# Mixer work of a fused attention and mixer kernel: eight single bursts into four double ones, and low-rank sums at another place

## The chip, the cores and the metric

One core of one Trainium2 chip. The metric is device time of one launch in microseconds (us); the kernel before takes 1078.82 us, the median of 3 runs (1078.75 to 1081.77; with the fourth run that came with the result, 1079.48). The gate for "faster" or "slower" is 2%.

## The reference

Two parts, one after the other, for 8 batches of 3136 rows and 256 columns, float32 in and out:

```python
scores = (1.0 / S) * np.matmul(z, z.transpose(0, 2, 1))   # z: 3136 x 64
out    = u * np.matmul(np.maximum(scores, 0.0) ** 2, v)   # attention
x      = out
h      = x.transpose(0, 2, 1) @ U @ V                     # mixer: rank 32 over the rows
u2     = x + h.transpose(0, 2, 1)
result = u2 + np.maximum(u2 @ w_ch1, 0.0) @ w_ch2         # 256 -> 1024 -> 256
```

## The kernel before

Rows come in 25 tiles of 128 (the last one of 64). Scores are symmetric, so only half of them are made: `A[j]` holds them, and the transposed other half (a `strip`) is made by a DMA transpose that SyncE (SP) issues four outputs ahead. The attention of batch b runs over 25 "outputs" i = 0 to 24. Two neighbouring outputs are a pair that shares two PSUM banks (where the matmuls write their sums; one for the upper, one for the lower 64 rows of the contraction); pairs alternate between two sets of banks. In the first half a pair is (0,1), (2,3) up to (10,11); output 12 is alone; then (13,14), (15,16) and so on.

Into the attention of batch b the kernel weaves the mixer of batch b-1 and prepares batch b+1: its z is loaded, doubled (VectorE), and transposed in two halves by SP, and its first scores are made. The mixer's steps are: `rank` once (x times U); for each of 7 chunks of four tiles (some have three or two) a `low_rank` step, which adds V's part to x and transposes the sum into `ut`; then "bursts". Burst n holds the first layer (`up`) of chunk n and the second layer (`down`) of chunk n-1.

The parts that the change touches, with cuts marked:

```python
    def spare():                       # the PSUM set that no open pair is using
        return sets[(opened[0] + (0 if acc else 1)) % 2]
    # ...
    def close_pair(b, o):              # ... = cut
        nc.scalar.copy(out=both[:, :w], in_=banks[1][:, :w])
        nc.vector.tensor_tensor(out=both[:, :w], in0=banks[0][:, :w], in1=both[:, :w], op=ALU.add)
        nc.vector.tensor_tensor(out=x_at(b, t0, n), in0=..., in1=u_sb..., op=ALU.mult)
    # ...
    def low_rank(b, c, ps=None):
        ps = spare() if ps is None else ps
        for (h, k), t in order:
            mm(out=ps[h][:, k * D : (k + 1) * D], lhsT=V_bf[halves[h], ...], rhs=t1[b][halves[h], :], ...)
        for h in range(2):
            nc.vector.tensor_tensor(out=q, in0=split(ps[h]...), in1=q, op=ALU.add)      # x += h
        transpose(out=ut..., in_=x...)                                                  # issued by SP
    # ... the main loop, batch b, output i:
        burst_at = dict(zip((2, 4, 6, 8, 10, 13, 15, 17), range(NC + 1)))
        z_load, z_double, z_half, z_turn = (1, 5, 7, 11) if b else (None, 9, 11, 13)
        ahead = dict(zip((1, 2, 4, 6, 8, 10, 13), range(NC)))
        for i in range(begin, NT):
            fill = ...                  # score steps of this batch and of the next one
            # ... z of batch b+1: load, double, turn in two halves, extend
            main = attend_steps(b, o)   # 25 steps of one output
            if b and i in ahead:
                main.insert(NT * 2 // 5, lambda c=ahead[i]: low_rank(b - 1, c))
            _spread(main, fill)         # score steps evenly between the steps of main
            if i + AHEAD < NT:
                turn(b, turns(i + AHEAD))           # strip for the output four later
            # ...
            if b and i == 0:
                rank(b - 1)
            if b and i in burst_at:
                up, down = bursts[burst_at[i]]
                # ... (the last batch keeps some for the end)
                run(_merge(down, up))   # alternates the steps of the two lists
```

The order of the instructions on each engine is the order of this program; engines wait for each other through semaphores only.

## Time and profile before

| | before |
|---|---|
| median time | 1078.82 us |
| span of the profiled run | 1078.5 us, granted clock (the share of full speed that the throttle allowed TensorE) 0.986 |
| TensorE busy | 94% |
| from one `rank` to the next, batches 2 to 6 | 126.8 to 127.1 us |

Three views of the page. First the busy shares and the chain that ended last:

```profile
...
PE 1010.8 (94%) x13789; PEld 792.3 (73%) x13829; DVE 525.7 (49%) x937; ACT 611.7 (57%) x814; POOL 179.0 (17%) x332
...
PE 77%; DVE 7%; DMA 6%; ACT 5%; issue 3%; POOL 1%; SPq 0%; POOLq 0%; ACTq 0%; DVEq 0%
PE ps L333 40%; PE ps L486 15%; PE ps L455 15%; PE ps L260 5%; ACT A L273 3%; DVE x_bf L435 2%; DMA strip<-A 2%; DVE both L348 2%; DVE A L275 2%; DMA ut<-x_bf 1%; DMA zT<-z_bf 1%; PE ps L401 1%; DVE x_bf L351 1%; ACT both L347 1%; PE ps L421 1%
...
```

TensorE is busy nearly throughout and holds 77% of the chain, so time is what TensorE computes plus what it waits. Busy time hides short waits, because the ends of matmuls are modelled; so I read the matmul records of the trace from start to start. A pair of 64-row matmuls with 256 columns takes 109 ns, a matmul of 512 columns 216 ns; what exceeds this is a loss. In a steady batch (2 to 6; I number the stretches between the `rank` steps by the batch whose attention runs, 1 to 7) the losses are:

| loss per steady batch, us | before |
|---|---|
| 16 changes between attention and burst, two of them with 0.26 us of other waits | 1.78 |
| 4 low-rank steps that wait for a bank | 1.83 |
| opening of output 2 behind low-rank step 0 | 0.58 |
| inside the first burst, for relus | 0.53 |

Two of them (the waits for a bank, L421, and the opening, L333 for L435) in the waits view, with three waits for transfers (engine and line, for whom; us in total, times, longest us):

```profile
...
PE ps L260 <- DMA zT<-z_bf: 20.3, 2, 10.2
...
PE ps L421 <- DVE both L348: 8.3, 28, 0.4
...
PE ps L455 <- DMA ut<-x_bf: 6.7, 3, 3.9
...
PE ps L333 <- DMA strip<-A: 3.9, 2, 2.3
...
PE ps L333 <- DVE x_bf L435: 2.3, 7, 0.3
...
```

L421 is the low-rank matmul: 28 times it waited for L348, the add that empties a bank. The view gives less than start to start (8.3 us against 7 x 1.83 = 12.8), since it counts from the modelled end of the matmul before. The two waits for zT are at the start and in batch 0, none in a steady batch. Why not is seen in SP's timeline around outputs 10 and 11 of one batch (start, length, queue and line, operation):

```profile
...
573.98 1.23 SPq L438 DMA_TRANSPOSE ut<-x_bf  x1
575.30 1.48 SPq L295 DMA_TRANSPOSE strip<-A  x1
576.87 2.16 SPq L184 DMA_TRANSPOSE zT<-z_bf  x1
...
```

and in TensorE's at the same time:

```profile
...
573.63 1.04 PE L455 MATMUL ps<-ut,w_bf 128*128 128x512 bf16 x3
...
579.82 1.59 PE L333 MATMUL ps<-v,A 64*128 64x256 bf16 x26
...
```

SP issues in order: the transpose of low-rank step 5, a strip, then the second half of the next batch's z (L184), at 576.87. It landed 4.9 us later, at 581.8. The burst ran from 573.63 to 579.82, so the three issues stood beside it; the first score of the next batch, in output 13, came at 585.8, 4.0 us after the landing.

### The profile page before, as it was taken

What the parts mean: (1) busy time and instruction counts of PE and PEld (TensorE: products, weight loads), DVE (VectorE), ACT (ScalarE), POOL (GpSimd) and SP (SyncE); (2) the same over time, 40 slices, a digit from 0 to 9 for tenths busy, and PEclk for the clock granted to TensorE, in tenths of its full rate; (3) what the DMA queues carried; (4) which work ended last, traced back from release to release, by engine and by line L of the source; (5) the groups of instructions that cost most, each with busy time, mean ns of one, the idle gap of its engine ahead of it and who ended that gap; (6) DMA issues with size and microseconds to landing.
All of it is one profiled execution on the core that took longest, in us unless ns stands there. A gap on an engine that the chain in (4) does not pass through costs nothing.

```text
span 1078.5 us, 31056 instructions
## 1 busy us (share of the span) xinstructions
PE 1010.8 (94%) x13789; PEld 792.3 (73%) x13829; DVE 525.7 (49%) x937; ACT 611.7 (57%) x814; POOL 179.0 (17%) x332
## 2 busy tenths in 40 slices
PE   5876989999999999999999999999999999999896
PEld 3665857788677877778777886778777887778564
DVE  4755734456443554446454465435554465432331
ACT  5955655466664666556654666556655566542253
POOL 3022201211121111211212111211112110111011
PEclk9998989999999999999999999999999999999898
DMA  8799999969989798979989789997989887588231
GB/s 142 145 170 190 172 163 169 172 140 169 162 173 176 150 183 163 164 159 167 177 167 173 147 167 160 175 179 150 179 158 171 168 160 134 129 150 168 57 98 64
DMA packets 417174, 168.71 MB, mean 156 GB/s; under 512 B 392768, under 2 KB 402640, under 8 KB 417040
## 3 DMA queue, kind: packets, MB, share of 16 engines
q1 hardware_dynamic: 386464, 96.77, 56.7%
q0 software_dynamic: 30576, 69.96, 27.7%
q8 instruction: 108, 1.77, 0.7%
q14 instruction: 26, 0.21, 0.1%
HBM read 61.88 MB, written 25.69 MB: 81 GB/s over the span
## 4 chain that ended last, share of the span: by engine, by line
PE 77%; DVE 7%; DMA 6%; ACT 5%; issue 3%; POOL 1%; SPq 0%; POOLq 0%; ACTq 0%; DVEq 0%
PE ps L333 40%; PE ps L486 15%; PE ps L455 15%; PE ps L260 5%; ACT A L273 3%; DVE x_bf L435 2%; DMA strip<-A 2%; DVE both L348 2%; DVE A L275 2%; DMA ut<-x_bf 1%; DMA zT<-z_bf 1%; PE ps L401 1%; DVE x_bf L351 1%; ACT both L347 1%; PE ps L421 1%
## 5 line engine op out<-in xcount | busy, mean ns | idle before, releaser
L273 ACT ACTIVATE A<-ps 128x832 bf16<-128x832 f32 (+8 forms) x469 | 351.6, 763 | 184.8 <-PE ps L260 175.5
L333 PE MATMUL ps<-v,A 64*128 64x256 bf16 x5064 | 357.9, 270 | 5.7 <-DVE x_bf L435 2.3
L275 DVE TENSOR_TENSOR A<-A 128x832 bf16<-128x832 bf16 (+8 forms) x469 | 240.5, 524 | 219.1 <-ACT A L273 216.2
L333 PE MATMUL ps<-v,strip 64*128 64x256 bf16 x4612 | 319.3, 269 | 3.9 <-DMA strip<-A 3.9
L462 ACT ACTIVATE relu<-ps 128x1024 bf16<-128x1024 f32 (+2 forms) x224 | 203.5, 917 | 190.5 <-PE ps L455 190.5
L333 PEld LDWEIGHTS <-A 64*128 64x128 bf16 x5064 | 251.5, 94 | 64.0 <-issue 27.3
L333 PEld LDWEIGHTS <-strip 64*128 64x128 bf16 x4612 | 233.3, 94 | 37.8 <-DMA strip<-A 4.5
L455 PE MATMUL ps<-ut,w_bf 128*128 128x512 bf16 (+2 forms) x856 | 205.1, 357 | 11.6 <-DMA ut<-x_bf 6.7
L486 PE MATMUL ps<-w_bf,relu 128*128 128x256 bf16 x1600 | 205.9, 273 | 1.0
L486 PEld LDWEIGHTS <-relu 128*128 128x128 bf16 x1600 | 153.8, 98 | 49.5 <-issue 9.3
L260 PE MATMUL ps<-zT 64*128 64x416 bf16 (+9 forms) x933 | 155.7, 317 | 23.3 <-DMA zT<-z_bf 20.3
L497 DVE TENSOR_TENSOR o_sb<-ps,x_bf 128x512 f32<-128x512 f32 (+1 forms) x104 | 69.7, 670 | 221.2 <-PE ps L486 221.2
L455 PEld LDWEIGHTS <-w_bf 128*128 128x128 bf16 x896 | 87.2, 99 | 69.6 <-issue 18.0
L317 POOL DMA_DIRECT2D u_sb<-in_u_dram x96 | 53.5, 558 | 494.3 <-DVE x_bf L351 440.7
L504 POOL DMA_DIRECT2D out_dram<-o_sb x96 | 52.4, 546 | 330.9 <-DVE o_sb L497 330.9
L347 ACT COPY both<-ps 128x512 f32<-128x512 f32 (+1 forms) x104 | 58.8, 566 | 64.7 <-PE ps L333 64.6
L348 DVE TENSOR_TENSOR both<-ps,both 128x512 f32<-128x512 f32 (+1 forms) x104 | 69.3, 666 | 53.0 <-ACT both L347 52.5
L260 PEld LDWEIGHTS <-zT 64*128 64x128 bf16 x933 | 53.1, 95 | 32.1 <-DMA zT<-z_bf 20.6
L351 DVE TENSOR_TENSOR x_bf<-both,u_sb 128x512 bf16<-128x512 f32 (+1 forms) x104 | 69.8, 671 | 6.3 <-DMA u_sb<-in_u_dram 2.7
L435 DVE TENSOR_TENSOR x_bf<-ps,x_bf 128x512 bf16<-128x512 f32 (+1 forms) x112 | 65.4, 625 | 15.4 <-PE ps L421 15.3
L195 POOL DMA_DIRECT2D v<-in_v_dram x61 | 34.1, 566 | 0.0
L421 PE MATMUL ps<-t_sb,V_bf 64*128 64x256 bf16 x200 | 22.6, 273 | 9.9 <-DVE both L348 8.3
(33 smaller groups left out, 134.2 us busy)
## 6 DMA issues: line engine op xcount, KB each, us to landing
u_sb<-in_u_dram POOLq DMA_DIRECT2D x96, 256.0 KB, 3.5
out_dram<-o_sb POOLq DMA_DIRECT2D x96, 256.0 KB, 3.0
v<-in_v_dram POOLq DMA_DIRECT2D x57, 192.0 KB, 5.9
strip<-A SPq DMA_TRANSPOSE x196, 4.9
z_c<-in_z_dram POOLq DMA_DIRECT2D x7, 384.0 KB, 5.5
w_bf<-in_moe_w_ch_dram POOLq DMA_DIRECT2D x2, 512.0 KB, 7.8
u_sb<-in_u_dram POOLq DMA_DIRECT2D x16, 64.0 KB, 2.2
ut<-x_bf SPq DMA_TRANSPOSE x56, 3.5
```

The costliest lines, as they stand in the source:

```text
L260: mm(out=ps[:, k, :n], lhsT=zT[halves[k], j, :], rhs=zT_flat[halves[k], c : c + n], start=True, stop=True,)
L273: nc.scalar.activation(out=dst, in_=src, func=AF.Relu, scale=sc)
L275: nc.vector.tensor_tensor(out=dst, in0=dst, in1=dst, op=ALU.mult)
L333: mm(out=acc[t0][h][:, (o - t0) * D : (o - t0 + 1) * D], lhsT=w[halves[h]], rhs=v_both[b % 2][halves[h], j, :], start=start, stop=stop, **kw,)
L347: nc.scalar.copy(out=both[:, :w], in_=banks[1][:, :w])
L348: nc.vector.tensor_tensor(out=both[:, :w], in0=banks[0][:, :w], in1=both[:, :w], op=ALU.add)
L351: nc.vector.tensor_tensor(out=x_at(b, t0, n), in0=split(both[:, :w]), in1=u_sb[:, :n, :].rearrange("p t (a c) -> p t a c", c=P), op=ALU.mult,)
L435: nc.vector.tensor_tensor(out=q, in0=split(ps[h][:, : len(ks) * D]), in1=q, op=ALU.add)
L455: mm(out=ps[:, i, :w], lhsT=w1_bf[:, db, (hp + i) * P : (hp + i + 1) * P], rhs=uT[c][:, db, len(chunks[c]) * P - w :], start=(db == 0), st ...
L462: nc.scalar.activation(out=relus[c][:, hp : hp + 2, :w], in_=ps[:, :, :w], func=AF.Relu)
L486: mm(out=ps[:, k * D : (k + 1) * D], lhsT=relus[c][:, ht, q : q + P], rhs=w2_bf[:, ht, :], start=(ht == 0), stop=(ht == NH - 1),)
L497: nc.vector.tensor_tensor(out=o_sb[:p, :nk, :].rearrange("p t (a c) -> p t a c", c=P), in0=split(ps[:p, : nk * D]), in1=x_at(b, t, nk)[:p] ...
```

## The change

Its intent: halve the number of changes between attention and burst, by running bursts in twos; begin each with a first-layer step, so that the second layer does not stand right behind the relu that it needs; and run the low-rank steps later in their outputs, when the bank they need has been emptied.

```diff
-        burst_at = dict(zip((2, 4, 6, 8, 10, 13, 15, 17), range(NC + 1)))
+        burst_at = {4: (0, 1), 8: (2, 3), 13: (4, 5), 17: (6, 7)}
...
-        ahead = dict(zip((1, 2, 4, 6, 8, 10, 13), range(NC)))
+        ahead = dict(zip((1, 2, 5, 6, 10, 11, 14), range(NC)))
...
-                main.insert(NT * 2 // 5, lambda c=ahead[i]: low_rank(b - 1, c))
+                main.insert(NT // 3 if i == 1 else NT * 2 // 3, lambda c=ahead[i]: low_rank(b - 1, c))
...
-            if b and i in burst_at:
-                up, down = bursts[burst_at[i]]
-                if not more and burst_at[i] >= NC - 1:
-                    late += up + (down if burst_at[i] == NC else [])
-                    up, down = [], (down if burst_at[i] < NC else [])
-                run(_merge(down, up))
+            for n in burst_at.get(i, ()) if b else ():
+                up, down = bursts[n]
+                if not more and n >= NC - 1:
+                    late += up + (down if n == NC else [])
+                    up, down = [], (down if n < NC else [])
+                run(_merge(up, down))
```

## The prediction

> **What bounds the kernel now.** TensorE: the page shows 94% busy, and PE lines hold 77% of the chain that ended last. I read the timeline of a steady batch (126.8 us) by its matmuls' starts. Beyond the streaming spacing (a 64-row pair of 256 columns 109 ns, a 512-column matmul 216 ns) TensorE loses:
> - mode changes: attention runs 64-row matmuls, mixer bursts 128-row ones. Each entry costs 93 ns extra (202 instead of 109), each exit 96. The Trainium skill, "TensorEngine Tiling (Array Packing)", Key Properties, says that changing the tiling mode drains TensorE; the trace agrees, with these numbers.
> - two burst entries wait 0.12 and 0.14 more.
> - low-rank sums at two fifths of an output wait for the spare PSUM pair, which the previous pair's copy and add still read (the waits name DVE both): 0.53, 0.54, 0.34, 0.42 us, 1.83 per batch.
> - after the low-rank step in output 1 (second of its pair) the next pair opens in the same PSUM banks and waits 0.58 us for the low-rank adds.
> - the lone first burst waits 0.5 us for ACT's relus.
>
> **What the change removes**, per batch: four of eight bursts (4 x 0.19 = 0.76), the entry waits (0.26), the low-rank waits (1.83; evacuation ends about 1.8 us into an output, two thirds lies at 1.9 or later). Together 2.85 us, all on TensorE's path.
>
> **What it adds.** Low-rank steps 2, 4 and 6 move to outputs 5, 11 and 14, each second of a pair: their sums land in the banks that the next output opens, a third of an output later. The DVE adds (0.64 us each) queue behind score squares; the skill, "TensorE: Matmul & The Clock Gate", table at its head, calls VectorE strict FIFO, and the trace agrees in order. My estimates from these durations:
> - output 6 opens 1.2 us late (VectorE has a burst's output, two z copies of 0.98 us, a square, then the adds);
> - output 12: 0.7; output 15: 0.9;
> - at the joint of the first double burst, 0.3 more for relus.
> - z transposition: its second half is issued on SP behind the low-rank transpose of output 10 and a strip, 7.1 us after output 10 opens, and lands 4.9 us later. Now a 5.9 us burst between outputs 10 and 11 hides it. Without it the first score of the next batch (output 13) comes before the landing: a wait of about 1.7 us.
>
> Added: 4.8 us, 1.7 in the last batch (no z work).
>
> **Sum.** Six batches at +2.0, the last at -1.0: about +11 us. Start and tail hardly change. Prediction 1088 us, 1078 to 1097. Faster by over 2%: 0.02; within: 0.91; slower: 0.07.
>
> **What the profile would show.** Half the burst entries and exits, still 93 to 96 ns each; waits of L421 for DVE both nearly gone; new waits of L333 for DVE x_bf (L435) at the openings after the moved steps, 15 to 20 us in total; waits of L260 (and DVE zT) for the zT transpose once per batch, absent now in steady batches; PE busy share lower.
>
> **What would make it wrong.** If the z transpose issues earlier than I reckon, the result is 1076 to 1080; if DVE reaches the low-rank adds before the score squares, openings wait little and it is 1065 to 1070. If strips and loads crowd the DMA engines (already about 90% busy) between bursts, it nears 1100.

## The result, and the profile after

1112.32 us, median of 4 runs (1109.17 to 1117.28), against 1079.48 us (1078.75 to 1081.77): ratio 1.0305, 95% interval 1.026 to 1.035. That is slower by more than 2%, and outside the predicted range of 1078 to 1097. A ratio here is the mean time of one kernel's fast runs over that of the other's of the same rounds, so it is not quite the ratio of the medians that I quote.

The page after:

```profile
...
PE 1023.2 (92%) x13829; PEld 822.1 (74%) x13829; DVE 528.1 (47%) x937; ACT 614.4 (55%) x814; POOL 179.3 (16%) x332
...
PE 77%; DMA 9%; DVE 5%; ACT 4%; issue 3%; POOL 1%; SPq 0%; POOLq 0%; ACTq 0%; DVEq 0%
PE ps L333 42%; PE ps L486 14%; PE ps L455 13%; PE ps L260 6%; DMA zT<-z_bf 4%; DMA strip<-A 4%; DVE x_bf L435 3%; ACT A L273 2%; ACT relu L462 1%; PE ps L401 1%; DVE z_bf L177 1%; DVE A L275 1%; PE ps L421 1%; POOL out_dram L504 0%; DMA v<-in_v_dram 0%
...
```

The chain now has zT and strip with 4% each among its lines. The waits:

```profile
...
DVE zT L189 <- DMA zT<-z_bf: 50.5, 8, 15.1
...
PE ps L260 <- DMA zT<-z_bf: 41.2, 8, 10.9
...
PE ps L333 <- DVE x_bf L435: 11.8, 33, 0.4
...
PE ps L333 <- DMA strip<-A: 4.3, 3, 1.9
...
PE ps L455 <- DMA ut<-x_bf: 2.7, 1, 2.7
...
```

Waits of L421 for the bank are gone, as predicted; L333 waits for the low-rank adds (L435) at openings, 33 times instead of 7, as predicted (11.8 us in this view, below the 15 to 20 of the prediction; the view counts from modelled ends, the ledger below from start to start); and L260, the score matmul, waits 6 times more for zT, as predicted, but for 41.2 - 20.3 = 20.9 us, where I had 10. The same place as before, SP around outputs 10 and 11 of one batch:

```profile
...
590.66 1.23 SPq L438 DMA_TRANSPOSE ut<-x_bf  x1
591.99 3.01 SPq L295 DMA_TRANSPOSE strip<-A  x1
595.10 1.60 SPq L184 DMA_TRANSPOSE zT<-z_bf  x1
596.78 2.57 SPq L438 DMA_TRANSPOSE ut<-x_bf  x1
...
```

The order on SP's queue is low-rank transpose, strip, z, as before, but now with no burst beside it. The z transpose was issued at 595.10 and landed 5.3 us later. TensorE meanwhile:

```profile
...
595.82 1.03 PE L333 MATMUL ps<-v,A 64*128 64x256 bf16 x15
600.48 0.20 PE L260 MATMUL ps<-zT 64*128 64x64 bf16 x2 [3.63 <-DMA zT<-z_bf]
600.52 0.71 PE L333 MATMUL ps<-v,A 64*128 64x256 bf16 x10
601.07 1.46 PE L333 MATMUL ps<-v,strip 64*128 64x256 bf16 x14
602.32 0.31 PE L260 MATMUL ps<-zT 64*128 64x128 bf16 x2
602.42 1.27 PE L333 MATMUL ps<-v,strip 64*128 64x256 bf16 x10
603.49 0.42 PE L333 MATMUL ps<-v,A 64*128 64x256 bf16 x2
603.84 1.46 PE L455 MATMUL ps<-ut,w_bf 128*128 128x512 bf16 x4
...
```

The last matmul before the wait started at 596.6, the first score at 600.48; the trace's records put 3.79 us between where it could have started and where it did. Then look at the lengths. Fourteen strip matmuls at 601.07 take 1.46 us; fourteen A matmuls in the profile of before take 0.93. Start to start, a pair takes 207 ns and not 109, and a 512-column matmul 427 ns and not 216. The windows view tells why (columns: window, its length, busy time and instructions of PE, PEld, DVE, ACT, POOL, then the granted clock, the DMA share, GB/s):

```profile
...
590.00:596.00 6.00, 5.67 (x103) 5.13 (x99) 3.84 (x7) 0.84 (x2) 2.38 (x5) 1.00 0.96 154
596.00:600.00 4.00, 0.85 (x16) 0.57 (x12) 0.00 (x0) 0.37 (x1) 0.00 (x0) 1.00 1.11 210
600.00:604.00 4.00, 3.52 (x41) 2.43 (x42) 1.75 (x5) 0.66 (x2) 0.55 (x1) 0.66 1.17 230
604.00:608.00 4.00, 4.00 (x26) 2.47 (x25) 0.42 (x1) 1.95 (x2) 0.55 (x1) 0.91 0.86 187
...
```

TensorE was busy 0.85 of 4 us, and in the next 4 us its granted clock is 0.66. The Trainium skill, "TensorE: Matmul & The Clock Gate", Part 1, says that the array's clock falls to half after an idle window of about 3.4 us that runs freely. The six waits of this run were 2.96, 3.76, 3.62, 3.79, 3.37 and 3.71 us; the last four were followed by slow matmuls, the first two not. The trace agrees with a window that runs freely, and the clock records of the packed trace show it: all changes of the granted clock in this run lie whole multiples of 3.413 us apart. Laid on that grid, the six waits put at most 1.97, 1.96, 3.41, 2.58, 2.15 and 2.47 us of their idle time into one window; where it was 2.15 or more, half clock began as that window ended (from 1.25 us before to 0.84 us after the end of the wait), and where it was 1.97 or less, it did not. So it was not the length of the wait that decided, and the window did not have to be idle throughout. This is read from traces; no run tried it on purpose. (The trace of before has the same once: after its one wait of 4.1 us in batch 1, for `ut`, the 512-column matmuls come at 427 ns. I had taken those for part of the start.) I had read that page and cited it for VectorE's queue, and did not ask what a wait of over 3 us would do to the clock.

The ledger. Periods of the stretches from `rank` to `rank`:

| us | start to first `rank` | batch 1 | 2 | 3 | 4 | 5 | 6 | 7 | rest |
|---|---|---|---|---|---|---|---|---|---|
| before | 126.1 | 132.88 | 126.84 | 127.05 | 126.82 | 126.83 | 126.83 | 119.78 | 65.3 |
| after | 137.3 | 129.66 | 130.52 | 133.05 | 132.18 | 132.81 | 133.14 | 118.69 | 65.1 |

Batches 2 to 6 gained 27.3 us in sum, 5.5 each. Their losses, means of the five:

| loss per steady batch, us | before | after | difference | predicted |
|---|---|---|---|---|
| changes between attention and burst | 1.78 | 0.75 | -1.03 | -1.02 |
| low-rank steps waiting for a bank | 1.83 | 0 | -1.83 | -1.83 |
| openings behind low-rank adds (outputs 2, 6, 12, 15) | 0.58 | 2.97 | +2.39 | +2.8 |
| first burst, for relus | 0.53 | 0.88 | +0.35 | +0.3 |
| wait for zT in output 13 | 0 | 3.65 | +3.65 | +1.7 |
| slow matmuls after that wait | 0 | 1.66 | +1.66 | not foreseen |
| a strip, in batch 3 alone | 0 | 0.20 | +0.20 | only as a risk |

The differences add up to 5.4, against 5.5 in the periods. Without the two zT lines and the strip the change comes out at -0.1 us per batch: what it saves, its new openings take back. Batch 7 prepares no z and gained 1.1 us, as predicted (1.0). The stretch up to the end of batch 1 lost 7.9 us (259.0 to 266.9), of which I had predicted 2. Up to the first `rank` the two programs are the same, and fourteen profiles (these two and the twelve of the experiments, none of which touches this stretch) differ there between 123 and 137 us, so one profile cannot tell what of this is chance; the experiments come back to it.

### The profile page after: what moved, and what is told of

It reads as the page before. It is cut to its first block, busy times and chain, and to the rows that moved or that the text cites. A ratio compares the mean times of both kernels' runs of the same rounds, so it can differ in the third digit from the quotient of the medians.

```text
span 1112.5 us, 31092 instructions
## 1 busy us (share of the span) xinstructions
PE 1023.2 (92%) x13829; PEld 822.1 (74%) x13829; DVE 528.1 (47%) x937; ACT 614.4 (55%) x814; POOL 179.3 (16%) x332
## 4 chain that ended last, share of the span: by engine, by line
PE 77%; DMA 9%; DVE 5%; ACT 4%; issue 3%; POOL 1%; SPq 0%; POOLq 0%; ACTq 0%; DVEq 0%
PE ps L333 42%; PE ps L486 14%; PE ps L455 13%; PE ps L260 6%; DMA zT<-z_bf 4%; DMA strip<-A 4%; DVE x_bf L435 3%; ACT A L273 2%; ACT relu L462 1%; PE ps L401 1%; DVE z_bf L177 1%; DVE A L275 1%; PE ps L421 1%; POOL out_dram L504 0%; DMA v<-in_v_dram 0%
## 5 line engine op out<-in xcount | busy, mean ns | idle before, releaser
L333 PE MATMUL ps<-v,A 64*128 64x256 bf16 x5064 | 358.2, 273 | 15.4 <-DVE x_bf L435 11.8
L333 PE MATMUL ps<-v,strip 64*128 64x256 bf16 x4612 | 335.3, 273 | 4.3 <-DMA strip<-A 4.3
L275 DVE TENSOR_TENSOR A<-A 128x832 bf16<-128x832 bf16 (+8 forms) x469 | 243.0, 524 | 172.6 <-ACT A L273 170.3
L333 PEld LDWEIGHTS <-A 64*128 64x128 bf16 x5064 | 269.4, 95 | 57.5 <-issue 29.6
L462 ACT ACTIVATE relu<-ps 128x1024 bf16<-128x1024 f32 (+2 forms) x224 | 202.7, 917 | 151.2 <-PE ps L455 151.0
L333 PEld LDWEIGHTS <-strip 64*128 64x128 bf16 x4612 | 250.6, 95 | 32.8 <-DMA strip<-A 5.1
L260 PE MATMUL ps<-zT 64*128 64x416 bf16 (+9 forms) x933 | 163.9, 322 | 50.1 <-DMA zT<-z_bf 41.2
L486 PE MATMUL ps<-w_bf,relu 128*128 128x256 bf16 x1600 | 204.7, 273 | 0.0
L486 PEld LDWEIGHTS <-relu 128*128 128x128 bf16 x1600 | 156.2, 98 | 46.6 <-issue 1.8
L260 PEld LDWEIGHTS <-zT 64*128 64x128 bf16 x933 | 59.5, 96 | 59.8 <-DMA zT<-z_bf 43.2
L348 DVE TENSOR_TENSOR both<-ps,both 128x512 f32<-128x512 f32 (+1 forms) x104 | 69.3, 667 | 25.7 <-ACT both L347 25.3
L435 DVE TENSOR_TENSOR x_bf<-ps,x_bf 128x512 bf16<-128x512 f32 (+1 forms) x112 | 65.5, 626 | 21.9 <-PE ps L421 21.9
L189 DVE COPY zT<-zT 128x1536 bf16<-128x1536 bf16 x8 | 4.5, 560 | 50.5 <-DMA zT<-z_bf 50.5
```

The costliest lines, as they stand in the source:

```text
L260: mm(out=ps[:, k, :n], lhsT=zT[halves[k], j, :], rhs=zT_flat[halves[k], c : c + n], start=True, stop=True,)
L275: nc.vector.tensor_tensor(out=dst, in0=dst, in1=dst, op=ALU.mult)
L333: mm(out=acc[t0][h][:, (o - t0) * D : (o - t0 + 1) * D], lhsT=w[halves[h]], rhs=v_both[b % 2][halves[h], j, :], start=start, stop=stop, **kw,)
L435: nc.vector.tensor_tensor(out=q, in0=split(ps[h][:, : len(ks) * D]), in1=q, op=ALU.add)
L462: nc.scalar.activation(out=relus[c][:, hp : hp + 2, :w], in_=ps[:, :, :w], func=AF.Relu)
L486: mm(out=ps[:, k * D : (k + 1) * D], lhsT=relus[c][:, ht, q : q + P], rhs=w2_bf[:, ht, :], start=(ht == 0), stop=(ht == NH - 1),)
```

## The experiments

Theory A: the loss is the late z transpose. It is late because the burst between outputs 10 and 11, which hid it, is gone; the wait also slows the clock after it (A2). Rivals: the double bursts crowd the transfers altogether (B); the moved low-rank steps put their transposes ahead of z's (C). Twelve kernels, in three calls; each call has its own runs of the kernel before.

### First scores behind the burst of output 13

```diff
-    next_at = ahead_of([max(NB, FIRST + j) for j in range(FIRST)], ...)
+    next_at = ahead_of([max(15, FIRST + j) for j in range(FIRST)], ...)     # NB is 13
```

> The changed kernel, with the first scores of the next batch moved from outputs 13 and 14 to output 15, behind the burst of output 13, so that they come after the landing of the transposed z. Theory A (the late z transpose is nearly the whole loss: a wait of 3.0 to 3.8 us per batch and the half-speed matmuls after it, together about 5.2 us in six batches): no wait for zT in steady batches, batch period back from 132-133 us to about 127, time 1081 us (1077 to 1086). Rival B (the double bursts crowd the transfers, so that strips or other tiles come late and the wait only shows at zT first): another wait appears in its place and the time stays above 1100.

Measured: 1084.67 us (1080.41 to 1089.74), ratio to before 1.0048 (0.9999 to 1.0098). In the waits:

```profile
...
PE ps L260 <- DMA zT<-z_bf: 20.3, 2, 10.4
...
PE ps L333 <- DMA strip<-A: 17.1, 8, 6.9
...
PE ps L333 <- DVE x_bf L435: 9.2, 27, 0.4
...
```

The zT waits are those of the start alone (2, as before), and 28 us of the 33 are gone: theory A for the steady batches. The openings fell from 11.8 to 9.2 us too: the adds before output 15 come earlier. But the expectation of B was not all wrong: strips now wait 17.1 us, 6.9 at once. That one is in batch 1:

```profile
...
142.97 0.60 PE L333 MATMUL ps<-v,strip 64*128 64x256 bf16 x7
150.47 0.39 PE L333 MATMUL ps<-v,strip 64*128 64x256 bf16 x1 [6.90 <-DMA strip<-A]
...
```

Steady batches were not spared: from start to start, batches 3, 5 and 6 wait 1.9, 1.6 and 2.2 us for a strip, and batches 2 to 6 take 126.3 to 129.6 us, 127.7 in the mean, where about 127 was expected. The 2.2 us wait in batch 6 lay within one window of the grid, and from 792 to 795 us, right after it, the granted clock is 0.50: a wait well below 3 us was enough.

### Useless matmuls in the place of the wait

```diff
+                if b and i == NB:
+                    def warm(score=fill[0]):
+                        ps = pair_psum()
+                        for _ in range(30):          # 30 row-tiled pairs, never read
+                            for h in range(2):
+                                mm(out=ps[:, h, :D], lhsT=V_bf[halves[h], :P], rhs=v_both[b % 2][halves[h], 0, :], ...)
+                        score()
+                    fill[0] = warm
```

> The changed kernel with 60 useless matmuls (30 row-tiled pairs, about 3.3 us) just before the first score of the next batch, where TensorE otherwise waits 3.0 to 3.8 us for zT; their result is never read. Theory A2[...]: the matmuls after the wait come at 109 ns per pair and not 207, time about 1104 us (1101 to 1107), although work was added. Rival: the slow matmuls come from something else (reads of data just landed, say): they stay at 207 ns and the time stays at 1112 or grows.

Measured: 1106.85 us (1101.86 to 1110.89), ratio 1.0238 (1.0181 to 1.0295). The same place, in the same batch:

```profile
...
599.65 3.45 PE L707 MATMUL ps<-v,V_bf 64*128 64x256 bf16 x60
603.46 0.20 PE L260 MATMUL ps<-zT 64*128 64x64 bf16 x2 [0.36 <-DMA zT<-z_bf]
603.50 0.71 PE L333 MATMUL ps<-v,A 64*128 64x256 bf16 x10
604.05 0.93 PE L333 MATMUL ps<-v,strip 64*128 64x256 bf16 x14
604.81 0.22 PE L260 MATMUL ps<-zT 64*128 64x128 bf16 x2
...
605.62 0.60 PE L455 MATMUL ps<-ut,w_bf 128*128 128x512 bf16 x2
```

Theory A2 is that the idle wait slows the clock. Fourteen strip matmuls take 0.93 us where they took 1.46 after the idle wait. Batches 3 to 6, the ones with slow matmuls in the change, take 130.4 to 130.7 us, against 132.2 to 133.1 there. So the slow matmuls come from standing idle, not from the data that has just landed. Batch 2, which had none in the change, takes 132.9 against 130.5: z landed even later than the useless matmuls lasted, and TensorE waited 2.1 us more. Batch 1 waits 9.9 us for a strip. By the times alone the step from 1112.32 is not secure, as the two ratios' intervals (1.018 to 1.030 and 1.026 to 1.035) overlap; the trace decides.

### The z transpose one output earlier

```diff
-        z_load, z_double, z_half, z_turn = (1, 5, 7, 11) if b else (None, 9, 11, 13)
+        z_load, z_double, z_half, z_turn = (1, 5, 7, 10) if b else (None, 9, 11, 13)
...
-    for j, i in enumerate((6, 7, 8, 9, 10, 10, 4, 2, 9, 8, 7, 6)):       # own score panels: none may still
+    for j, i in enumerate((6, 7, 8, 9, 3, 5, 4, 2, 9, 8, 7, 6)):         # read the old z at output 10
```

> The changed kernel with the second half of the z transpose issued at output 10 in place of 11, that is ahead of the low-rank transpose of output 10 in SP's queue (the two score panels that still read the old z at output 10 are made at outputs 3 and 5). Theory A' (z comes late because it stands behind that transpose and a strip in SP's in-order queue, and those wait for VectorE): z lands about 7 us earlier, no zT wait, time 1083 us (1078 to 1089). Rival (the DMA engines themselves are too full between the bursts): z still lands late, the wait only shrinks, above 1095.

Measured: 1087.05 us (1084.08 to 1091.54), ratio 1.0081 (1.0011 to 1.015).

```profile
...
PE ps L260 <- DMA zT<-z_bf: 20.1, 2, 10.2
...
PE ps L333 <- DVE x_bf L435: 17.1, 37, 1.5
...
PE ps L333 <- DMA strip<-A: 12.0, 3, 8.6
...
```

No zT wait in a steady batch, with the first scores left at output 13. In batches 2 to 6 z was issued 56.5 us after `rank`, in the change 64.4 to 65.9, and it landed 4.5 to 6.4 us after its issue, no faster than before. So it was its place in SP's in-order queue that made z late, not the transfer itself. The batch-1 strip wait is there again (8.6 us). The opening waits rise to 17.1 us: in batch 4 VectorE stands idle 2.7 us at L189, the copy that needs z, and the low-rank adds behind it come late (1.5 us).

### Double bursts alone

The change with `ahead` and the place in the output as in the kernel before.

```diff
-        ahead = dict(zip((1, 2, 5, 6, 10, 11, 14), range(NC)))
+        ahead = dict(zip((1, 2, 4, 6, 8, 10, 13), range(NC)))
-                main.insert(NT // 3 if i == 1 else NT * 2 // 3, ...)
+                main.insert(NT * 2 // 5, ...)
```

> The changed kernel with the low-rank steps back at their old outputs and at two fifths; only the double bursts and their order are left of the change. Theory A (the burst that stood between outputs 10 and 11 hid the z transpose; its removal exposes it): a zT wait of 3 us or more per batch with the slow matmuls after it, some -5 us for fewer mode changes, about 1104 us (1097 to 1111). Rival C (the moved low-rank steps, two of them in outputs 10 and 11, put their transposes ahead of z's): no zT wait, 1072 to 1078.

Measured: 1122.8 us (1117.99 to 1124.31), ratio 1.0392 (1.035 to 1.0435): slower than the change itself, and above the 1097 to 1111 that I gave.

```profile
...
PE ps L260 <- DMA zT<-z_bf: 48.9, 8, 9.9
...
PE ps L333 <- DMA strip<-A: 10.1, 4, 6.1
PE ps L421 <- DVE both L348: 8.3, 28, 0.4
...
```

Rival C falls: with the low-rank steps at their old outputs the zT waits are longer (48.9 us in the view, 4.0 to 7.6 us each), with the slow matmuls after them, and the low-rank waits of before are there as well. I had again taken a zT wait of about 3 us plus 2.

### Low-rank place alone

The kernel before with single bursts and the old outputs; only the place within the output and the order of the merge are the change's.

```diff
-                main.insert(NT * 2 // 5, ...)
+                main.insert(NT // 3 if i == 1 else NT * 2 // 3, ...)
-                run(_merge(down, up))
+                run(_merge(up, down))
```

> The kernel before with single bursts and the old outputs for the low-rank steps, but each low-rank step at two thirds of its output (a third in output 1) and bursts beginning with a first-layer step. Theory: the waits of the low-rank sums for the bank being evacuated (1.83 us per batch) vanish and nothing comes back, since no low-rank step moved into the second output of a pair: 1066 us (1063 to 1070). Rival: the wait returns, at the burst's entry or in DVE's queue: 1074 to 1080.

> The kernel with single bursts at the old outputs, low-rank steps at two thirds and bursts begun with a first-layer step, again with more rounds beside the others of this call: 1068 us (1066 to 1071); the run with doubles that keep 2 and 10 should be some 2 us below it on the same chip.

Measured: 1068.13 us (1067.59 to 1073.36), ratio 0.9904 (0.9864 to 0.9944), and again, with five rounds on another chip, 1070.35 us (1064.07 to 1073.22), ratio 0.9929 (0.9904 to 0.9954). Steady batches take 125.55 us and have no low-rank wait and no zT wait. This part of the change is good by itself, by close to 1%.

### Low-rank steps on first outputs of pairs

The first experiment's kernel (first scores at output 15), and:

```diff
-        ahead = dict(zip((1, 2, 5, 6, 10, 11, 14), range(NC)))
+        ahead = dict(zip((1, 2, 4, 6, 8, 10, 15), range(NC)))
```

> As the run that moved the first scores of the next batch to output 15, and also low-rank steps 2 to 6 moved to outputs 4, 6, 8, 10, 15, each the first of its pair, still at two thirds. Theory: the openings of outputs 6 and 12 no longer wait for the low-rank adds (2.0 us per batch down to 0.5, in seven batches 10.5 us) and no wait of the low-rank sums returns: 1074 us (1070 to 1079). Rival (the opening waits are covered elsewhere, or the low-rank waits come back): 1082 or more.

Measured: 1071.43 us (1068.43 to 1078.18), ratio 0.9942 (0.988 to 1.0004).

```profile
...
PE ps L333 <- DMA strip<-A: 6.3, 2, 4.5
...
PE ps L486 <- DVE both L348: 5.7, 6, 1.5
...
PE ps L333 <- DVE x_bf L435: 2.3, 7, 0.3
...
```

The opening waits are back to the 2.3 us of before, and steady batches take 125.3 to 126.4 us. What the moved steps cost is this: a low-rank step in the second output of a pair uses the banks that the next output opens. A new, smaller wait shows for L486: second-layer steps whose bank waits for L348, 0.7 to 1.7 us per batch. The trace shows where it comes from: in each of the six batches VectorE has stood idle 5.7 to 6.6 us at L189 until z landed, and L348 is its next instruction. So a late z still costs something, through VectorE.

### Order of the merge

The kernel of the run before this, with `_merge(down, up)`.

> The run with first scores at 15 and low-rank steps on first outputs (1071), with the merge of each burst turned back to second layer first. Theory: at each joint of a double burst the second layer now waits for the last relu of the step just before it (about 0.5 us at three joints, 0.4 more at the first), and at output 8 its first step waits for the low-rank adds in its bank (0.8 us): 2.5 to 3 us per batch, 1089 us (1084 to 1093). Rival (the relus keep up): 1070 to 1074.

Measured: 1090.24 us (1084.06 to 1093.25), ratio 1.0117 (1.0091 to 1.0143). The waits view has a line of L486 waiting for the relus of L462, 21 times, which the kernel of the run before lacks. So "begun with a first-layer step" is worth some 18 us where bursts are doubled (1090.24 against 1071.43, from different calls); without it the double bursts would have cost yet more.

### A burst back at output 2

Two runs: on the kernel of low-rank steps on first outputs, and on the first experiment's kernel.

```diff
-        burst_at = {4: (0, 1), 8: (2, 3), 13: (4, 5), 17: (6, 7)}
+        burst_at = {2: (0,), 4: (1,), 8: (2, 3), 13: (4, 5), 17: (6, 7)}
```

> As the run with first scores at 15 and low-rank steps on first outputs, but the first double burst taken apart: burst 0 at output 2, burst 1 at output 4. Theory S (with no burst before output 4 the first steady batch waits 7 to 10 us for a strip, because the transposes after the start are slow; a burst at output 2 covers it, with a shorter wait for the first transposed group as in the kernel before): the strip wait in that batch shrinks to 5 us or less, for 1.1 us more of mode changes: 3 to 5 us faster than that run, about 1070. Rival (the strip wait is a loss of the start that comes out anywhere): no difference, or 1 us slower.

> The run with first scores at output 15 only (1084.7), with burst 0 back at output 2 and burst 1 at output 4; nothing else. Theory S: the 7 us strip wait of the first steady batch goes or shrinks to under 2 us, against 1.1 us of mode changes: 1079 us (1076 to 1082). Rival: the wait comes out elsewhere at the start, 1084 or more.

Measured: the first 1069.91 us (1068.46 to 1071.28), ratio 0.9919 (0.9866 to 0.9972), against 0.9942 without the burst at 2; the second 1077.76 us (1069.71 to 1082.69), ratio 1.0002 (0.9967 to 1.0037), against 1.0048. Both point the same way, and both pairs of intervals overlap, so the times do not settle it. The traces say more. With no burst at output 2, six of the seven kernels (first scores at 15, useless matmuls, z earlier, bursts alone, first outputs, down first) wait 4.6 to 9.9 us for a strip in batch 1; the seventh, the change itself, stood 6.5 us at the end of batch 0 instead, where an activation waited for a strip to be read. With a burst at output 2 (before, the two low-rank runs, these two, and the last run) none does; but before and the low-rank runs wait 3.7 to 4.1 us for the first `ut` there. In the mean the stretch up to the end of batch 1 is some us longer without that burst; how many, in a stretch that varies by 14 us between profiles, stays open.

### Doubles at other places

One run of these gave a wrong result: windows at 2 (0), 6 (1, 2), 10 (3, 4), 13 (5), 17 (6, 7), with low-rank steps at the old outputs.

> Low-rank steps at the old outputs and two thirds, bursts begun with a first-layer step, and double bursts only where they leave a burst at outputs 2 and 10: windows at 2 (0), 6 (1, 2), 10 (3, 4), 13 (5), 17 (6, 7). Theory: the z transpose stays hidden behind the burst of output 10, the first strips of a batch behind that of output 2, and three windows fewer save 3 x 0.19 us in six batches against the run with single bursts (1068): 1064.5 us (1062 to 1068). Rival (four outputs in a row without a burst already starve the strips): strip waits, 1069 or more.

Measured: relative error 0.27; 1066.22 us (1061.15 to 1068.59). Chunk 0's second layer in burst 1 reads x in a buffer that batch b overwrites at the end of output 5; at output 6 it is too late. This follows from the code; it is an error of program order, not a race. Its time tells nothing of a usable kernel. The last run keeps burst 1 at output 4:

```diff
+        burst_at = {2: (0,), 4: (1,), 8: (2, 3), 10: (4,), 13: (5,), 17: (6, 7)}
+        ahead = dict(zip((1, 2, 4, 6, 8, 10, 13), range(NC)))
```

> Low-rank steps at the old outputs and two thirds, bursts begun with a first-layer step, windows at 2 (0), 4 (1), 8 (2, 3), 10 (4), 13 (5), 17 (6, 7): the doubles that keep a burst at outputs 2 and 10 and keep every group's last read ahead of its overwriting. Theory: no zT wait, no long strip wait, two windows fewer than the run with single bursts, so about 2.3 us below it: 1065 us (1062 to 1069), correct. Rival: a strip or sum waits in the stretch of outputs 5 to 8, 1070 or more.

Measured, correct: 1063.87 us (1057.88 to 1066.72), ratio 0.9871 (0.9845 to 0.9898) to before; the low-rank run has 0.9929, and the intervals do not meet.

```profile
...
PE ps L260 <- DMA zT<-z_bf: 18.0, 2, 10.2
...
```

Steady batches take 124.7 to 125.1 us against 125.55. Of these 0.9 us, two windows fewer give 4 x 0.095 = 0.38, and 0.42 is a wait in the single burst of output 8 for the low-rank adds in its bank, which the double does not have. I had expected 2.3 us between the two kernels; the medians differ by 6.5. It is the fastest of the correct kernels here, though still "same" by the 2% gate, 1.3% below before and 4.4% below the change (1063.87 against 1112.32, from different calls).

## Why the prediction was wrong

- **What bounds the kernel**: right. The losses from start to start added up in both traces.
- **What is removed** (2.85 us per batch): right. Measured 1.03 + 1.83 = 2.86.
- **Openings of outputs 6, 12 and 15**: right in kind; predicted 1.2, 0.7, 0.9, measured in one batch 1.02, 0.55, 0.82. (By the code the step at output 11 is low-rank step 5; step 4, which the prediction names, goes to output 10, the first of its pair.) VectorE's order was as foreseen: burst output, two z copies, square, adds. Putting the steps on first outputs removed it.
- **The joint of the first double burst**: predicted 0.3, measured 0.35.
- **The step that failed**: the term "a wait of about 1.7 us" for z. The mechanism was right, down to the output: issued behind the low-rank transpose of output 10 and a strip, hidden before by the burst, exposed without it. The size was off twice. (a) The wait was 3.65 us in the mean. I had taken the strip's issue as 1.48 us, as it lasted beside a burst; in the change the strip issue at that place took 3.1, 3.0 and 3.3 us in batches 2, 4 and 6, in batches 3 and 5 the `ut` issue before it took 2.5 instead of 1.2, and landing took 5.0 to 5.3 instead of 4.9. The other traces bear out that this goes with the burst: in the four kernels with a burst at output 10 that ran correctly (before, the two low-rank runs and the last run) that strip's issue took 1.45 to 1.51 us in all 24 batches, while the kernel of bursts alone, with low-rank steps where they were before, had 2.99 us or more in five of six. (The run with the wrong result, a double burst at output 10, had 1.45 to 3.24.) Why it takes longer there no run shows. (b) The prediction stopped at the end of the wait. After such waits TensorE ran at half clock for some us in four of the six batches: 1.5 to 2.6 us each, which the useless matmuls took away. Six waits sum to 21.2 us and the slow stretches to 8.3, together 29.5, where I had 6 x 1.7 = 10.2. These 19.3 us alone carry 1088 to 1107.
- **The start**: I wrote "Start and tail hardly change". The profile has 7.9 us more up to the end of batch 1, where I had 2. In part this is chance (up to 14 us between profiles of an identical stretch), and in part, it may be, transfers that come late with no burst at output 2; the times do not settle it. I had named something like it, "if strips and loads crowd the DMA engines ... between bursts, it nears 1100"; in the steady batches it took 1 us in one of five.
- **The chances**: I gave 0.07 to slower by 2%. My own list had one term, the z wait, that depends on two durations taken from a trace in which a burst gave the queue room; a range that allowed for that term should have been wider upward.

## What to carry to other kernels

A block of pure TensorE work does two jobs: it computes, and it gives transfers and other engines time; before moving it, list for each queue what lands during it, and who needs that next. Durations measured beside such a block are not those without it. And when a predicted wait of TensorE comes to 2 us or more, reckon with a slow clock after it: here waits of 2.2 to 3.8 us could bring one, depending on how they lay on the grid of windows, and in the change each one cost 1.5 to 2.6 us.

## What the Trainium skill lacked or had wrong

- "TensorEngine Tiling (Array Packing)", Key Properties: it says that a change of tiling mode drains TensorE but gives no cost. Here it is 93 ns going in (202 against 109) and 96 ns coming out, per change.
- "TensorE: Matmul & The Clock Gate", Part 1: right in the size of the loss (it puts the ramp at under 1% of a typical kernel's span, and 8.3 of 1112.5 us is 0.7%), but it gives no loss for one wait in a stream of row-tiled pairs; its worked case is another kernel. Here it is 1.5 to 2.6 us after a wait of 3.4 to 3.8 us. Where it speaks of an idle window, the window need not be idle throughout: 2.15 us of idle time within one of 3.41 us was enough, 1.97 was not, so waits of 2.96 and 3.76 us that fell across two windows went without half clock.
- "DMA: Bandwidth & Descriptors": I found no figure there, said to be of this chip, for how long the issue of one DMA transpose holds SP's queue. Here a strip takes 1.3 us at the least, 1.5 in the median and up to 7.2 before; the one ahead of z took 1.3 to 1.5 us beside a burst and 3.0 to 3.3 in three of six batches without one, and everything behind it waits.
